# Thresholding one chunk a pair on Pool, and transposing the last queries on TensorE, in the opening of an attention and gated MLP kernel

## The chip, the cores and the metric

The kernel runs on one core of one Trainium2 chip. The metric is the device time of one execution in microseconds. The profile is one execution under the hardware profiler; its span is the time from its first to its last instruction, some 1.8 us shorter than the device time of the same execution.

A core has TensorE (PE in the profile; PEld are its weight loads), VectorE (DVE), ScalarE (ACT), GpSimd (POOL) and SyncE (SP, which issues most of the DMAs here). I write PE, Vector, Scalar and Pool. PE's results land in PSUM; e, the masks and the numerators of this kernel are in SBUF.

## The reference

```python
# attention: q, k, v are (8, 8, 576, 64); tau = 0.02
scores = scale * q @ k.T                        # 576 x 576 for each of 64 heads
scores = where(scores >= max(scores) - tau, scores, -1e9)
attn   = exp(scores - max(scores)); attn /= sum(attn)
x      = attn @ v                               # to (8, 576, 512)
# gated MLP with a spatial product
h = relu(x @ w_in); u, v = halves of h
v_n = normalise(v); v_s = w_spatial @ v_n + b
out = (u * v_s) @ w_out
```

An exponential is kept where it is at least exp(-tau), and is zero otherwise. That is the threshold. The kept values are the numerators.

## The kernel before

The 64 heads are worked through as 32 pairs. A pair has four chunks of 128 queries (c = 0 to 3), and its last 64 queries are put together with those of its neighbour as chunk 4 of the odd pair. So two pairs make nine steps, and there are 144 steps. A step computes the scores of one chunk (128 x 1152: two heads of 576 keys), takes the maximum, and exponentiates; the threshold of a chunk is applied one step later. The second half of the work, the MLP, enters at step 26. What comes before I call the opening, and what follows the body; the prediction counts pair 6 (steps 27 to 30) still to the opening.

```python
def on_act(c):
    return c in (2, 4)            # these chunks are thresholded by Scalar

def mask():                       # the chunk of the step before
    i, c, e = unmasked.pop()
    if c == 4:                    # last queries of two pairs
        dst = pts[i // 2] = ptr_ring[i // 2 % 2]
        nc.sync.dma_start_transpose(out=dst, in_=pr_ring[i // 2 % 2])
        return
    pt = p_ring[2 * (i % 2) + c // 2]
    if not on_act(c):             # chunks 0, 1, 3: Vector, e is fp32 in SBUF
        ef = e.rearrange("p h s -> p (h s)")
        nc.vector.scalar_tensor_tensor(out=pt[:, c % 2, :], in0=ef, scalar=ctau, in1=ef,
                                       op0=ALU.is_ge, op1=ALU.mult)
    if c % 2:                     # two chunks: numerators transposed by a DMA
        ...dma_start_transpose...

def step(i, c, fs):
    s = scores(i, c)              # PE into one of two PSUM score buffers
    ...                           # PE's and Scalar's small work of the step, fs[:2]
    nc.vector.tensor_reduce(out=nm, in_=s, axis=AX.X, op=ALU.max, negate=True)
    if on_act(c):                 # the bias instruction: 2 columns, SBUF to SBUF
        nc.vector.tensor_scalar(out=nm, in0=nm, scalar1=by, scalar2=float(tau),
                                op0=ALU.mult, op1=ALU.add)
    ...                           # Vector's divisions of fs[:2]
    e = ep.tile([P, 2, S], F32, name="e")       # ep has bufs=3
    ...                           # Scalar: exponentials of both heads from s into e
    if unmasked:
        mask()
    unmasked.append((i, c, e))
    ...                           # fs[2:]
```

Pool copies loaded q, k and v into working layouts, makes a small block-diagonal key tile (kd), and in the body normalises v.

## Time and profile before

| | before |
|---|---|
| three runs | 479.87 us (479.84 to 483.53) |
| span of the profile | 478.6 us |
| PE busy | 448.3 us, 94% |
| Vector busy | 418.0 us, 87% |
| Scalar busy | 382.2 us, 80% |
| Pool busy | 229.1 us, 48% |
| numerators to their transposes on the DMA queue, last queries | 16 transposes, 3.7 us each from issue to landing |

Busy time says how long an engine's instructions were under way, including the time in which a started instruction waits (the bias instruction shows 0.17 us in one place of this trace and 1.07 us in another, where Pool works at the same time).

### The profile page before, as it was taken

The numbers are of one execution on the slowest core, as the hardware profiler recorded it, in microseconds if no ns is written. First come the engines' busy times: TensorE is split into PE (matmuls) and PEld (weight loads), VectorE is DVE, ScalarE is ACT, GpSimd is POOL, SyncE is SP. The second block draws the span as 40 slices with busy tenths as digits, with TensorE's granted clock in tenths as the row PEclk, the third lists the DMA queues.
The fourth block names the chain that finished last, engine by engine and source line by source line (L and its number), as shares of the span: only waits on it lengthen the run. The fifth ranks groups of instructions, "written<-read, shape, count | busy, mean of one in ns | idle before, by whom it ended". The sixth has DMA issues, their size and how long they took to land.

```text
span 478.6 us, 9894 instructions
## 1 busy us (share of the span) xinstructions
PE 448.3 (94%) x3664; PEld 238.3 (50%) x3664; DVE 418.0 (87%) x563; ACT 382.2 (80%) x666; POOL 229.1 (48%) x403
## 2 busy tenths in 40 slices
PE   7788888889899999999999999999999999999995
PEld 4344444454554555554555545555554545545542
DVE  4999999989889997999889898899889998898573
ACT  4778777998879798788979898798978889797251
POOL 3462544784337553474427652475436743253021
PEclk9899999999999999999999999999999999999999
DMA  7999999979999799898988999997996999766523
GB/s 225 255 185 199 223 236 197 214 159 204 179 191 194 172 212 223 189 170 183 192 197 202 182 200 191 223 190 156 222 227 170 195 173 218 138 113 120 149 82 117
DMA packets 231120, 89.38 MB, mean 187 GB/s; under 512 B 200608, under 2 KB 225312, under 8 KB 231072
## 3 DMA queue, kind: packets, MB, share of 16 engines
q1 hardware_dynamic: 230416, 87.86, 87.2%
q8 instruction: 29, 0.48, 0.4%
q0 software_dynamic: 160, 0.52, 0.3%
q10 hardware_dynamic: 496, 0.36, 0.2%
q14 instruction: 19, 0.16, 0.1%
HBM read 33.31 MB, written 9.44 MB: 89 GB/s over the span
## 4 chain that ended last, share of the span: by engine, by line
PE 48%; DVE 23%; ACT 19%; issue 6%; DMA 2%; SPq 1%; POOL 0%; POOLq 0%; ACTq 0%; DVEq 0%
PE s L550 14%; DVE negm L586 10%; DVE p L567 8%; PE f L245 5%; ACT e L609 5%; PE s L545 4%; ACT e L603 4%; PE f L294 4%; PE f L519 4%; PE f L460 3%; ACT p L605 2%; ACT vrel L428 2%; PE f L490 2%; PE f L289 2%; ACT sq L442 1%
## 5 line engine op out<-in xcount | busy, mean ns | idle before, releaser
L586 DVE TENSOR_REDUCE negm<-s 128x2 f32<-128x1152 f32 x144 | 194.8, 1353 | 26.1 <-PE s L550 25.3
L550 PE MATMUL s<-qkT 64*128 64x512 f32 (+1 forms) x640 | 162.9, 639 | 0.0
L567 DVE SCALAR_TENSOR_TENSOR p<-e,ctau 128x1152 bf16<-128x1152 f32 x96 | 138.6, 1444 | 1.3 <-ACT e L609 1.2
L609 ACT ACTIVATE e<-s,negm 128x576 f32<-128x576 f32 x192 | 131.8, 741 | 7.1 <-DVE negm L586 6.8
L603 ACT ACTIVATE e<-s,negm 128x576 f32<-128x576 f32 x96 | 65.9, 738 | 20.9 <-DVE negm L590 11.6
L545 PE MATMUL s<-kd,qkT 128*128 128x128 f32 (+1 forms) x320 | 64.4, 304 | 15.6 <-ACT e L609 10.5
L268 POOL COPY kd<-qkT 64x64 f32<-64x64 f32 x62 | 31.7, 512 | 91.2 <-ACT qkT L263 89.4
L545 PEld LDWEIGHTS s<-kd,qkT 128*128 128x128 f32 (+1 forms) x320 | 44.4, 180 | 34.7 <-ACT e L609 20.2
L550 PEld LDWEIGHTS s<-qkT 64*128 64x128 f32 (+1 forms) x640 | 42.1, 174 | 18.3 <-issue 3.0
L436 POOL TENSOR_SCALAR nmean<-sm 128x1 f32<-128x1 f32 (+1 forms) x35 | 15.3, 437 | 69.7 <-ACT vrel L428 64.3
L294 PEld LDWEIGHTS <-pT 128*128 128x128 bf16 x1024 | 41.8, 97 | 7.3 <-issue 4.8
L294 PE MATMUL f<-v,pT 128*128 128x65 bf16 x992 | 44.9, 194 | 0.0
L136 POOL COPY qn<-ql 128x640 f32<-128x640 f32 x31 | 34.7, 1120 | 21.2 <-DMA ql<-in_k_dram 15.1
L605 ACT ACTIVATE p<-e 128x1152 bf16<-128x1152 f32 x32 | 37.3, 1165 | 1.0
L252 ACT COPY qkT<-f 128x512 f32<-128x512 f32 x31 | 18.2, 587 | 16.4 <-PE f L245 16.4
L490 PE MATMUL f<-wsT,vn 128*128 128x512 bf16 x125 | 31.1, 379 | 0.0
L448 POOL TENSOR_SCALAR vn<-vrel,rs,nm 128x512 bf16<-128x512 f32 (+1 forms) x34 | 28.7, 844 | 3.7
L289 PE MATMUL f<-v,pT 128*128 128x130 bf16 x124 | 27.2, 219 | 3.5 <-ACT qkT L252 1.6
L460 PE MATMUL f<-xT,w_in 128*128 128x512 bf16 x112 | 28.7, 380 | 0.9 <-DVE xn L303 0.8
L418 PE MATMUL f<-w_in,xT 128*128 128x512 bf16 x112 | 28.8, 380 | 0.0
L303 DVE TENSOR_TENSOR xn<-f,r 128x256 bf16<-128x256 f32 x62 | 26.3, 425 | 2.1
L428 ACT ACTIVATE vrel<-f 128x512 f32<-128x512 f32 (+1 forms) x34 | 20.1, 592 | 7.6 <-PE f L418 5.2
(165 smaller groups left out, 638.7 us busy)
## 6 DMA issues: line engine op xcount, KB each, us to landing
vl<-in_v_dram SPq DMA_DIRECT2D x16, 512.0 KB, 4.4
ql<-in_q_dram SPq DMA_DIRECT2D x15, 512.0 KB, 4.6
kl<-in_k_dram SPq DMA_DIRECT2D x15, 512.0 KB, 4.5
out_dram<-o SPq DMA_DIRECT2D x20, 256.0 KB, 3.4
uT<-in_moe_w_in_dram SPq DMA_DIRECT2D x3, 512.0 KB, 6.6
uT<-in_moe_w_spatial_dram SPq DMA_DIRECT2D x2, 576.0 KB, 5.0
vl<-in_v_dram SPq DMA_DIRECT2D x16, 64.0 KB, 4.1
pT<-p SPq DMA_TRANSPOSE x64, 5.5
```

The costliest lines, as they stand in the source:

```text
L136: nc.gpsimd.tensor_copy(out=t, in_=ld_ring[i // 2 % 2][w][:, 2 * (i % 2):2 * (i % 2) + 2].rearrange("p h c d -> p c h d"))
L289: nc.tensor.matmul(out=t[:, at:at + 130], lhsT=pt[:, 4, :], rhs=vt[:, 4:6, :].rearrange("p b d -> p (b d)"), start=True, stop=False)
L294: nc.tensor.matmul(out=t[:, at + 65 * h:at + 65 * h + 65], lhsT=pt[:, 5 * h + j, :], rhs=vt[:, 6 * h + j, :], start=False, stop=(h == 1 an ...
L460: nc.tensor.matmul(out=t, lhsT=w_in[:, m, f * P:(f + 1) * P], rhs=xts[b][:, m, 0:512], start=(m == 0), stop=(m == 3))
L490: nc.tensor.matmul(out=t, lhsT=vn[:, c, f * P:(f + 1) * P], rhs=wsT[:, c, 0:512], start=(c == 0), stop=(c == 4))
L545: nc.tensor.matmul(out=view(s[rows], 512, [[448, 2], [1, 64]]), lhsT=qks[n][:, 0, m], rhs=kd_ring[n % 2], start=True, stop=True)
L550: nc.tensor.matmul(out=s[rows, 1024 * h:1024 * h + 512], lhsT=qks[n][hs, 0, m], rhs=qks[n][hs, 1, 0:512], start=True, stop=True)
L567: nc.vector.scalar_tensor_tensor(out=pt[:, c % 2, :], in0=ef, scalar=ctau, in1=ef, op0=ALU.is_ge, op1=ALU.mult)
L586: nc.vector.tensor_reduce(out=nm, in_=s, axis=AX.X, op=ALU.max, negate=True)
L603: nc.scalar.activation(out=e[:, h, :], in_=s[:, h, :], func=ACT.Prelu, bias=nm[:, h:h + 1], scale=by, alpha=1e30)
L605: nc.scalar.activation(out=pr_ring[i // 2 % 2] if c == 4 else p_ring[2 * (i % 2) + c // 2][:, c % 2], in_=e.rearrange("p h s -> p (h s)"), ...
L609: nc.scalar.activation(out=e[:, h, :], in_=s[:, h, :], func=ACT.Exp, bias=nm[:, h:h + 1])
```

## The change

Vector is busy 98% of the time from 40 to 80 us, while Pool is more than half idle (8.60 and 8.90 us busy of 20). The change takes the threshold of chunk 0 from Vector in pairs 1 to 6 and gives it to Pool. Where Vector compares and multiplies in one instruction, the change uses two on Pool: a comparison into a bf16 mask `keep`, and a product. The change also takes three DMA transposes (the last queries of pairs 0 to 5) off the queue and does them on PE, nine 128 x 128 blocks each, in two jobs with a Scalar eviction each.

```diff
+    keep = const.tile([P, 1152], BF16, name="keep")
...
+    def pr_pe(m, half):
+        n0, n1 = ((0, 5), (5, 9))[half]
+        ...
+        def mm():
+            t = hold["t"] = bank16()
+            for n in range(n0, n1):
+                nc.tensor.transpose(out=t[:, (n - n0) * P:(n - n0 + 1) * P],
+                                    in_=pr_ring[m % 2][:, n * P:(n + 1) * P], identity=identb)
+        def ev():
+            nc.scalar.copy(out=ptr_ring[m % 2][:, n0:n1, :].rearrange("p n s -> p (n s)"),
+                           in_=hold["t"][:, 0:(n1 - n0) * P])
+        return "act", mm, ev
...
+            if i // 2 in r_on_pe:
+                return
             nc.sync.dma_start_transpose(out=dst, in_=pr_ring[i // 2 % 2])
...
-        if not on_act(c):
+        if c == 0 and 0 < i < 7:
+            ef = e.rearrange("p h s -> p (h s)")
+            nc.gpsimd.tensor_scalar(out=keep, in0=ef, scalar1=ctau, scalar2=1.0,
+                                    op0=ALU.is_ge, op1=ALU.mult)
+            nc.gpsimd.tensor_tensor(out=pt[:, c % 2, :], in0=ef, in1=keep, op=ALU.mult)
+        elif not on_act(c):
...
+    r_on_pe = {0: (9, 11), 1: (18, 20), 2: (25, 27)}
...
```

More of the change, by code (lines that the diff above doesn't have):

```diff
@@ L379, in x_pe @@
         return "act", mm, ev
+    def pr_pe(m, half):
+        n0, n1 = ((0, 5), (5, 9))[half]
+        hold = {}
+        def mm():
[7 more added lines that the diff above has]
+        return "act", mm, ev
     def ws_pe(c):
@@ L767 @@
         jobs.setdefault((29, 33, 34, 42, 44)[j], []).append((ws_pe, j))
+    for m, gs_ in r_on_pe.items():
+        for half, g in enumerate(gs_):
+            jobs.setdefault(g, []).append((pr_pe, m, half))
     with tc.manual_schedule():
```

## The prediction

> **What bounds the kernel now.** I read the page's slices first, then busy time by stretches, then the order of instructions on Vector, Scalar and Pool in the stretch that the change touches.
>
> ```profile
> PE   7788888889899999999999999999999999999995
> DVE  4999999989889997999889898899889998898573
> ```
>
> A slice is 12 us. TensorE (PE) reaches nine tenths and stays there only from about 110 us; before that Vector (DVE) is at nine tenths and more. By stretches, columns being PE, PEld, DVE, ACT, POOL busy us, clock, DMA share, GB/s:
>
> ```profile
> 40.00:60.00 20.00, 16.52 (x150) 9.19 (x148) 19.64 (x26) 16.24 (x25) 8.60 (x13) 1.00 0.92 207
> 60.00:80.00 20.00, 16.79 (x159) 9.03 (x157) 19.64 (x25) 14.52 (x23) 8.90 (x13) 1.00 1.13 217
> ...
> 360.00:400.00 40.00, 39.48 (x322) 20.34 (x319) 37.34 (x47) 34.91 (x64) 23.97 (x42) 1.00 0.90 192
> ```
>
> From 24 to 91 us, which is pairs 1 to 6, Vector is busy 98% (19.64 of 20) and PE about 83%; later PE is at 99%. So the kernel is a Vector-bound opening, then a PE-bound body. The body's PE work does not depend on when it starts, so I count a shift of the opening's end as a shift of the end. What moves the opening is therefore the question. One pair of it, pair 4, on Vector (start, duration, what):
>
> ```profile
> 57.77 1.41 DVE L567 SCALAR_TENSOR_TENSOR p<-e,ctau 128x1152 bf16<-128x1152 f32 x1
> 59.10 1.36 DVE L586 TENSOR_REDUCE negm<-s 128x2 f32<-128x1152 f32 x1
> 60.37 1.41 DVE L567 SCALAR_TENSOR_TENSOR p<-e,ctau 128x1152 bf16<-128x1152 f32 x1
> 61.70 1.35 DVE L586 TENSOR_REDUCE negm<-s 128x2 f32<-128x1152 f32 x1
> 63.08 0.71 DVE L590 TENSOR_SCALAR negm<-negm 128x2 f32<-128x2 f32 x1
> 63.70 1.83 DVE L567 SCALAR_TENSOR_TENSOR p<-e,ctau 128x1152 bf16<-128x1152 f32 x1
> 65.45 1.34 DVE L586 TENSOR_REDUCE negm<-s 128x2 f32<-128x1152 f32 x1
> ```
>
> The threshold at 60.37 is the one of chunk 0 that moves to Pool; the reduce at 61.70 and the tiny bias instruction at 63.08 belong to chunk 2; the threshold at 63.70 is that of chunk 1. Pool in the same time:
>
> ```profile
> 59.67 0.53 POOL L268 COPY kd<-qkT 64x64 f32<-64x64 f32 x2 [4.80 <-ACT qkT L263]
> 63.05 0.72 POOL L136 COPY qn<-ql 128x640 f32<-128x640 f32 x1 [2.85 <-DMA ql<-in_k_dram]
> 63.71 0.61 POOL L136 COPY kn<-kl 128x512 f32<-128x512 f32 x1
> 64.27 1.84 POOL L156 CAST v<-vl 128x640 bf16<-128x640 f32 x1
> ```
>
> The reader is to see the exclusion. The bias instruction takes 0.17 us when Pool is idle, here 0.71: it ends at 63.79, when Pool's copy of 63.05 ends (63.77). The threshold at 63.70 takes 1.83 instead of 1.41, because Pool's next copy (63.71 to 64.32) got in first; Pool's cast at 64.27 then takes 1.84 instead of 0.72, because the threshold holds it up. Elsewhere the same: bias instruction 51.89 to 52.91 against a Pool cast 51.85 to 52.89; 77.00 to 78.07 against 76.96 to 78.04. A reduce, which reads PSUM, is 1.35 us whatever Pool does.
>
> **What the Trainium skill says.** "SBUF — State Buffer", section "SBUF: two separate sides": Vector and Pool share a port pair, an exclusive lock held for the whole instruction, against Vector operations in a two-port mode or with two SBUF inputs. The trace agrees, with the numbers just given. "GPSIMD Engine Reference", section 3.1 "Elementwise — side-by-side cycle accounting": a Pool tensor_tensor of 2048 fp32 elements took 4497 ns, 1.96 times Vector's. This trace has Pool tensor_tensors of a few elements only, so nothing here confirms it. "TensorE: Matmul & The Clock Gate", "Part 4: PE-mode transpose": it lands in PSUM and needs a copy after; 275 to 390 ns each. Here four bf16 transposes in a row (the first at 59.14) are followed 0.23 us later by other work, so for throughput I use 0.06 us each.
>
> **The change, part by part.**
>
> Removed from Vector: six thresholds, in pairs 1 to 6. Each is 1.41 us on record and 1.33 us to the next instruction's start (60.37 to 61.70), so 8.0 us: the most that this part can give, 1.7% of 479.87.
>
> Added to Pool: six comparisons and six products of 1152 columns. Comparison: Pool's two-operation tensor_scalar on 512 columns with nothing in its way is 0.77 us (94.24 us), on one column 0.19; that is 1.13 ns a column, so 0.19 + 1151 x 0.00113 = 1.50 us. Product, estimated from the skill's figure scaled by columns: 4497 x 1152/2048 = 2.53 us. With a hop of 0.05 us, 4.1 us a pair, 24.5 us in all. Pool has that time (8.9 busy of 20), but holds the lock in it.
>
> When does it run? Chunk 0's exponentials of pair 4 end at 59.26 (57.89 + 1.37). Then come Scalar's small eviction (59.34) and the two kd copies, done at 60.20; both stand ahead in program order. So Pool compares from 60.20 to 61.70 and multiplies from 61.75 to 64.30: the end is 5.05 us after the exponentials. And Vector? The scores of chunk 2 wait for those same exponentials (two score buffers), and their last matmul ends at 60.87, so with the threshold gone the reduce starts at 60.9, not 61.70: the chain of exponentials, scores and reduce gives only 0.8 of the 1.33 us. The reduce ends at 62.25; the bias instruction then meets the product in flight and waits to 64.30, where before it ended at 63.79. If it should slip in between the two Pool instructions, the threshold of chunk 1 waits to the same 64.30.
>
> So I compare, for each pair, 5.05 us with the time from the end of chunk 0's exponentials to the end of the bias instruction before: 3.87, 3.98, 4.29, 4.53, 4.35 and 3.99 us for pairs 1 to 6 (28.75 - 24.88, 39.10 - 35.12, 52.91 - 48.62, 63.79 - 59.26, 78.07 - 73.72, 88.41 - 84.42). They sum to 25.0; six times 5.05 is 30.3. **The Pool part thus costs about 5.3 us instead of gaining 8.**
>
> Transposes on PE: 27 x 0.06 = 1.6 us of PE in a stretch where it idles a sixth; near nothing. Their six evictions cost Scalar 0.60 us (640 columns, like wsT at 88.37, next start 0.59 later) or 0.48 (512 columns, like xT at 46.76), 3.2 us. Those at steps 11, 20 and 25 stand before an exponential that waits for the bias instruction, and are hidden. Those at steps 9, 18 and 27 stand between the q eviction and chunk 0's exponentials, which start at once now (eviction from 57.34, exponentials at 57.89): they delay these by 0.60 + 0.60 + 0.48 = 1.7 us.
>
> Removed from the DMA queue: three transposes of 1.3 us of issue each. The queue is full from 40 to 82 us, but what it brings is early: Pool copies qn of pair 6 at 63.05 and PE transposes it at 69.73. The waits of PE for pT are 5.0 us in five places over the whole run. I give it 0.5 us.
>
> Given back: from 91 us on Vector has idle gaps (0.22, 0.78, 1.00 us by 98.5), so pair 6's loss is partly absorbed: 1.5 us. Sum: 5.3 + 1.7 - 0.5 - 1.5 = +5.0 us.
>
> **The rivals.** First, Pool is quicker than the estimate. At 3.0 us for both instructions the end comes at 3.95 us, below the mean of the six (4.17), so the pairs gain 1.3 us together, and with the evictions the change comes out at about even. For it: the mask is bf16, and a plain Pool copy of 1024 columns takes 1.04 us, 1 ns a column; against it: a two-input operation. Second, the change does what it is meant to: Vector's 8 us come off, less the 0.5 us a pair that the score buffers keep, minus the 1.7 us of evictions, about 3.5 us: 476 us. It needs Pool to finish within 2.1 us, or the lock to be rarely met. For it: the choice of exactly these pairs and steps looks tuned. Third, Pool's backlog makes it worse: its copies of qn and kn (0.66 + 0.56 us) then stand ready just when the threshold of chunk 1 wants the lock, and win it as at 63.71. In four of six pairs that adds 0.66 each, 2.6 us: about 487.5 us; with a product of 3 us, 490 us. Fourth, the DMA queue is the real bound of the opening (share 1.13): then three issues of 1.3 us would give up to 4 us, 476 us again. Against it: in the chain of waits the opening runs over Vector's reduces and thresholds, with one DMA stretch, 3.94 us.
>
> **Range and chances.** From +5.0 us I take 0.4 off for the first two rivals against the third: 484.5 us. The low end, 477.0, is the second rival nearly in full; the high end, 490.5, the third with a slow product. Faster by 2% needs 470.3 us, more than the whole 8 us: 3%. Slower by 2% is 489.5 us: 14%. Within: 83%.
>
> **What would show it.** Right: Pool comparisons near 1.5 us and products near 2.5 us; the bias instruction of chunk 2 in pairs 1 to 6 lengthened from 0.2-1.1 us to 1-2 us, ending with the product; Vector's busy time in 40 to 80 us still high, but from waiting; the first reduce of pair 7 (92.66 us now) later by about 5 us; the rest of the span unchanged in length. Wrong: a product under 1.5 us, or bias instructions that end before it, or pair 7 starting early. If pair 7 starts later and the end does not, then the claim that the opening's shift passes through is what failed.

## The result, and the profile after

The changed kernel took 501.29 us (median of 4 executions, 499.13 to 501.8) beside 480.66 us of the kernel before (479.84 to 483.53). The ratio is 1.0409, with a 95% interval from 1.0354 to 1.0465. A ratio here is the mean time of one kernel's fast runs over that of the other's of the same rounds, so it is not quite the ratio of the medians. The change made the kernel 4.1% slower. I had predicted 484.5 us, with 490.5 as the upper end.

The page's slices of the changed kernel, a slice being 12.5 us now:

```profile
PE   7768787859989999999999999999999999999995
DVE  5897898866988998799988998899898998899573
...
PEclk9887988997999999999999999999999999999998
```

And of the kernel before, the clock line that the prediction did not show:

```profile
PEclk9899999999999999999999999999999999999999
```

Neither PE nor Vector is near full through the first nine slices, so something holds both. The granted clock is also lower there. By stretches, with the same columns as in the prediction (PE, PEld, DVE, ACT, POOL busy us, clock, DMA share, GB/s):

```profile
40.00:60.00 20.00, 16.89 (x148) 9.52 (x146) 15.89 (x19) 14.42 (x23) 12.92 (x11) 0.93 0.81 182
60.00:80.00 20.00, 15.14 (x110) 7.21 (x107) 17.58 (x17) 13.24 (x20) 17.35 (x14) 0.84 0.73 174
...
360.00:400.00 40.00, 39.25 (x332) 21.18 (x333) 35.24 (x48) 33.93 (x61) 20.76 (x38) 1.00 1.02 199
```

Vector ran 36 instructions in 40 to 80 us, where it ran 51 before; Pool is busy for 30.3 us of these 40, where it was for 17.5. From 360 us on the two kernels look alike. The tile `keep` and its readers tell why (duration min, median, max in ns):

```profile
L587 POOL TENSOR_SCALAR keep<-e,ctau x6: 4174/4176/4178, 27.5 to 103.6; 128x1152 bf16<-128x1152 f32 x6
L589 POOL TENSOR_TENSOR p<-e,keep x6: 2361/2752/3144, 31.8 to 107.9; 128x1152 bf16<-128x1152 f32 x6
```

The product is 2.36 us where nothing obstructs it, near the 2.53 us that I estimated. The comparison is 4.18 us, and I had put it at 1.50. Pair 4 on Vector and then on Pool, the same pair as in the prediction (start, duration):

```profile
69.61 1.36 DVE L611 TENSOR_REDUCE negm<-s 128x2 f32<-128x1152 f32 x1
71.95 1.36 DVE L611 TENSOR_REDUCE negm<-s 128x2 f32<-128x1152 f32 x1 [0.98 <-PE s L567]
73.34 2.00 DVE L615 TENSOR_SCALAR negm<-negm 128x2 f32<-128x2 f32 x1
74.90 1.41 DVE L592 SCALAR_TENSOR_TENSOR p<-e,ctau 128x1152 bf16<-128x1152 f32 x1
76.23 1.34 DVE L611 TENSOR_REDUCE negm<-s 128x2 f32<-128x1152 f32 x1
```

```profile
70.52 0.52 POOL L269 COPY kd<-qkT 64x64 f32<-64x64 f32 x2 [2.33 <-ACT qkT L264]
71.14 4.18 POOL L587 TENSOR_SCALAR keep<-e,ctau 128x1152 bf16<-128x1152 f32 x1
75.40 3.14 POOL L589 TENSOR_TENSOR p<-e,keep 128x1152 bf16<-128x1152 f32 x1
```

The bias instruction asks at 73.34, while the comparison is under way, and ends at 75.34, when the comparison has ended (75.32). The threshold of chunk 1 follows at once and gets in before Pool's product, which therefore takes 3.14 us. In pairs 1 and 3 it is the other way round, because Vector has a division to do between bias instruction and threshold. Pair 1, on Vector and on Pool:

```profile
27.70 4.01 DVE L615 TENSOR_SCALAR negm<-negm 128x2 f32<-128x2 f32 x1
31.28 0.44 DVE L302 RECIPROCAL r<-f 128x4 f32<-128x4 f32 x1
31.78 0.42 DVE L304 TENSOR_TENSOR xn<-f,r 128x256 bf16<-128x256 f32 x1
32.12 3.24 DVE L592 SCALAR_TENSOR_TENSOR p<-e,ctau 128x1152 bf16<-128x1152 f32 x1
```

```profile
27.52 4.18 POOL L587 TENSOR_SCALAR keep<-e,ctau 128x1152 bf16<-128x1152 f32 x1
31.78 2.37 POOL L589 TENSOR_TENSOR p<-e,keep 128x1152 bf16<-128x1152 f32 x1
```

Here the bias instruction waits for the whole comparison (27.70 to 31.71), the product starts at 31.78 while Vector divides, and the threshold waits for the product too, from 32.12 to 34.15.

To see where the time comes from, I take the start of Vector's maximum in each of the 144 steps in both traces and subtract. The shift of the changed kernel against the one before, in us, at the first maximum of a pair:

| | pair 1, chunk 1 | pair 2 | pair 3 | pair 4 | pair 5 | pair 6 | pair 7 | pair 8 | step 102 | last step |
|---|---|---|---|---|---|---|---|---|---|---|
| start in the kernel before | 24.3 | 32.4 | 42.2 | 56.5 | 67.3 | 81.7 | 92.7 | 109.2 | 311.9 | 437.7 |
| shift of the changed kernel | -0.3 | +4.7 | +7.4 | +10.5 | +12.1 | +13.8 | +13.6 | +19.7 | +19.6 | +20.2 |

All of it arises before pair 8, and from there it hardly changes: the spans differ by 20.8 us (499.4 - 478.6).

### The profile page after: what moved, and what is told of

It is laid out like the page before. It is cut to its first block, busy times and chain, and to the rows that moved or that the text cites. A ratio compares the mean times of both kernels' runs of the same rounds, so it can differ in the third digit from the quotient of the medians.

```text
span 499.4 us, 9898 instructions
## 1 busy us (share of the span) xinstructions
PE 457.5 (92%) x3646; PEld 243.9 (49%) x3691; DVE 420.2 (84%) x557; ACT 385.5 (77%) x672; POOL 263.1 (53%) x415
## 4 chain that ended last, share of the span: by engine, by line
PE 52%; ACT 19%; DVE 16%; issue 5%; POOL 4%; DMA 2%; SPq 0%; POOLq 0%; ACTq 0%; DVEq 0%
PE s L567 16%; DVE negm L611 7%; ACT e L634 6%; PE s L562 5%; DVE p L592 5%; PE f L246 5%; PE f L295 4%; ACT e L628 4%; PE f L536 4%; PE f L477 3%; DVE negm L615 3%; PE f L507 2%; PE f L435 2%; PE f L290 2%; POOL keep L587 2%
## 5 line engine op out<-in xcount | busy, mean ns | idle before, releaser
L567 PE MATMUL s<-qkT 64*128 64x512 f32 (+1 forms) x640 | 168.1, 659 | 0.0
L634 ACT ACTIVATE e<-s,negm 128x576 f32<-128x576 f32 x192 | 131.7, 741 | 14.7 <-POOL p L589 5.0
L592 DVE SCALAR_TENSOR_TENSOR p<-e,ctau 128x1152 bf16<-128x1152 f32 x90 | 133.3, 1481 | 4.3 <-ACT e L634 4.2
L562 PE MATMUL s<-kd,qkT 128*128 128x128 f32 (+1 forms) x320 | 66.1, 311 | 23.4 <-ACT e L634 11.8
L269 POOL COPY kd<-qkT 64x64 f32<-64x64 f32 x62 | 28.0, 452 | 85.6 <-ACT qkT L264 83.8
L562 PEld LDWEIGHTS s<-kd,qkT 128*128 128x128 f32 (+1 forms) x320 | 45.6, 184 | 42.0 <-ACT e L634 21.0
L567 PEld LDWEIGHTS s<-qkT 64*128 64x128 f32 (+1 forms) x640 | 43.4, 180 | 19.0 <-issue 4.4
L453 POOL TENSOR_SCALAR nmean<-sm 128x1 f32<-128x1 f32 (+1 forms) x35 | 14.7, 419 | 67.8 <-ACT vrel L445 67.6
L137 POOL COPY qn<-ql 128x640 f32<-128x640 f32 x31 | 38.3, 1235 | 16.3 <-DVE negm L615 6.0
L465 POOL TENSOR_SCALAR vn<-vrel,rs,nm 128x512 bf16<-128x512 f32 (+1 forms) x34 | 27.3, 803 | 3.7
L246 PEld LDWEIGHTS f<-identf,qn 128*128 128x128 f32 x124 | 14.2, 150 | 26.9 <-POOL v L161 8.3
```

The source lines that it names most:

```text
L137: nc.gpsimd.tensor_copy(out=t, in_=ld_ring[i // 2 % 2][w][:, 2 * (i % 2):2 * (i % 2) + 2].rearrange("p h c d -> p c h d"))
L246: nc.tensor.transpose(out=t[:, c * P:(c + 1) * P], in_=nat[i][which][:, c, :], identity=identf)
L562: nc.tensor.matmul(out=view(s[rows], 512, [[448, 2], [1, 64]]), lhsT=qks[n][:, 0, m], rhs=kd_ring[n % 2], start=True, stop=True)
L567: nc.tensor.matmul(out=s[rows, 1024 * h:1024 * h + 512], lhsT=qks[n][hs, 0, m], rhs=qks[n][hs, 1, 0:512], start=True, stop=True)
L634: nc.scalar.activation(out=e[:, h, :], in_=s[:, h, :], func=ACT.Exp, bias=nm[:, h:h + 1])
```

## The experiments

Twelve kernels ran. The table gives the time, the ratio to the kernel before in the same rounds with its 95% interval, and the shift at pair 7, pair 8 and the last step from the one profile of each, made as above. The kernel before had medians of 479.22, 479.89 and 480.53 us in the rounds of the a, b and c runs; the b runs were on another chip than the a and c runs, so I compare runs of different letters by their ratios. Shifts under about 1.5 us mean little: at chunk 1 of pair 1 the profiles already differ from that of before by -1.7 to +1.2 us, the +1.2 being in a1, whose transposes all come later.

| run | us | ratio | pair 7 | pair 8 | last |
|---|---|---|---|---|---|
| changed kernel | 501.29 | 1.0409 (1.0354 to 1.0465) | +13.6 | +19.7 | +20.2 |
| a1, transposes alone | 481.31 | 1.0040 (1.0020 to 1.0060) | +1.9 | +1.8 | +1.8 |
| a2, Pool alone | 503.69 | 1.0501 (1.0475 to 1.0527) | +21.0 | +23.7 | +23.5 |
| a3, six forms | 496.40, one run | none | +8.8 | +15.1 | +15.4 |
| a4, comparison read by nobody | 501.07, one of four slow | 1.0418 (1.0375 to 1.0462) | +20.1 | +20.0 | +19.8 |
| b1, quick first instruction | 487.87 | 1.0145 (1.0106 to 1.0184) | +4.3 | +6.8 | +8.8 |
| b2, one quick instruction | 481.01 | 1.0015 (0.9981 to 1.0049) | -2.1 | -1.9 | +1.5 |
| b3, without pair 6 | 494.73 | 1.0301 (1.0257 to 1.0344) | +13.0 | +12.9 | +12.7 |
| b4, split bias, changed kernel | 499.20 | 1.0389 (1.0355 to 1.0424) | +10.8 | +16.8 | +18.5 |
| c3, four e buffers, changed kernel | 496.66 | 1.0333 (1.0294 to 1.0372) | +11.3 | +14.7 | +13.9 |
| c2, split bias, kernel before | 480.72 | 1.0004 (0.9972 to 1.0036) | -1.2 | -1.3 | +0.4 |
| c1, chunk 0 on Scalar | 481.29 | 1.0007 (0.9971 to 1.0043) | +0.2 | +0.1 | +2.3 |
| c5, split and half on Scalar | 481.19 | 1.0008 (0.9982 to 1.0034) | -0.8 | -1.0 | +0.2 |

My theory after the result was that Pool's slow comparison, and the port lock that it holds against Vector, make the loss. The rivals were the transposes, the late numerators with the buffers they hold, and the lowered clock.

### a1: the transposes alone

```diff
-        if c == 0 and 0 < i < 7:
+        if False:
```

> The transposes on PE alone, all thresholds on Vector. My theory (Pool's comparison of 4.18 us and the lock that it holds make the loss): close to the kernel before, 479 to 482.5 us, because only the evictions at steps 9, 18 and 27 (0.60 + 0.60 + 0.48 us) stand in the chain and three DMA transposes go away. Rival (the transposes and their evictions carry a large part of the loss, or the lowered TensorE clock comes from them): 485 us or more.

It took 481.31 us, 0.4% over the kernel before, which is 1.9 us (479.22 x 0.0040). So the transposes are slightly harmful and carry no large part of the loss. Its profile shows +1.2 us already at chunk 1 of pair 1, before the first of these transposes, and a granted clock of 0.87 in 20 to 40 us, so the trace does not give the evictions their 1.7 us; the time agrees with my net of 1.2 us for this part (1.7 - 0.5) within its interval.

### a2: Pool's thresholds alone

```diff
-    r_on_pe = {0: (9, 11), 1: (18, 20), 2: (25, 27)}
+    r_on_pe = {}
```

> The Pool thresholds alone, transposes left on the DMA queue. My theory: nearly the whole loss, 497 to 502 us, with comparisons of 4.2 us and the bias instructions of chunk 2 waiting 2 to 4 us. Rival (the transposes carry much of it): under 493 us.

It took 503.69 us, above what I expected, and more than the whole change with both its parts. Nearly the whole loss is Pool's. The surplus arises in pairs 5 and 6. In the changed kernel the transpose job of step 25 pushes pair 5's division behind the threshold of chunk 1, so that the threshold follows the bias instruction directly and asks for the port before Pool's product does (91.16 us, 1.41 us long). Here the division stands in between and the threshold loses:

```profile
90.05 2.00 DVE L615 TENSOR_SCALAR negm<-negm 128x2 f32<-128x2 f32 x1
91.61 0.44 DVE L302 RECIPROCAL r<-f 128x4 f32<-128x4 f32 x1
92.11 0.42 DVE L304 TENSOR_TENSOR xn<-f,r 128x256 bf16<-128x256 f32 x1
92.45 3.25 DVE L592 SCALAR_TENSOR_TENSOR p<-e,ctau 128x1152 bf16<-128x1152 f32 x1
```

That explains some 2 us at pair 6 (+15.8 against +13.8). The rest, from pair 6 to pair 7, I have not taken apart.

### a3: which form is slow

The edit gives the first Pool instruction of each pair another form, in short:

```text
pair 1: op0=is_ge, op1=mult      (scalars: ctau, 1.0, as in the change)
pair 2: op0=mult, op1=add        (ctau, 1.0)
pair 3: op0=max, op1=mult        (ctau, 1.0)
pair 4: op0=is_ge                (ctau, no second operation)
pair 5: op0=is_ge, op1=mult      (the constant 0.9802, 1.0)
pair 6: op0=subtract, op1=mult   (ctau, ctau)
```

> Changed kernel with another first Pool instruction in each pair (results wrong on purpose): pair 1 is_ge then mult, pair 2 mult then add, pair 3 max then mult, pair 4 is_ge alone, pair 5 is_ge then mult with the threshold as a constant, pair 6 subtract then mult with two pointer scalars. Theory A (the comparison is what is slow on Pool): 4.2 us in pairs 1, 4 and 5, about 1.5 us in pairs 2, 3 and 6, time about halfway, 485 to 493 us. Theory B (1152 columns or the conversion to bf16 are slow, whatever the operation): 4.2 us in all six, time near 500 us. Theory C (max is slow like is_ge): pair 3 also 4.2 us.

The six first instructions on Pool, in order of pairs:

```profile
25.93 4.18 POOL L588 TENSOR_SCALAR keep<-e,ctau 128x1152 bf16<-128x1152 f32 x1
...
40.76 1.22 POOL L590 TENSOR_SCALAR keep<-e,ctau 128x1152 bf16<-128x1152 f32 x1
...
55.33 4.18 POOL L592 TENSOR_SCALAR keep<-e,ctau 128x1152 bf16<-128x1152 f32 x1
...
69.09 3.21 POOL L594 TENSOR_SCALAR keep<-e,ctau 128x1152 bf16<-128x1152 f32 x1
...
82.67 4.10 POOL L596 TENSOR_SCALAR keep<-e 128x1152 bf16<-128x1152 f32 x1
...
98.82 4.25 POOL L598 TENSOR_SCALAR keep<-e,ctau 128x1152 bf16<-128x1152 f32 x1
```

None of my three theories holds as I stated it (theory C had pair 3 right, but not pair 6). It is not the comparison: max then mult takes the same 4.18 us and subtract then mult 4.25. It is not the width or the conversion: mult then add takes 1.22 us on the same tiles. Of these six, only mult then add is quick, and that is exactly the form of the normalising instruction from which I had scaled. Leaving out the second operation brings 3.21 us. Each form stands here once, in one execution; mult then add comes again in b1, with 1.22 us in most pairs. Why the forms differ is not shown. Its output is wrong, which doesn't matter for the time.

### a4: a comparison that nobody reads

```diff
+        if c == 0 and 0 < i < 7:
+            nc.gpsimd.tensor_scalar(out=keep, in0=still, scalar1=ctau, scalar2=1.0,
+                                    op0=ALU.is_ge, op1=ALU.mult)
         if not on_act(c):              # kernel before; still is a fixed fp32 tile
```

> The kernel before, with all thresholds kept on Vector, and in pairs 1 to 6 one more Pool comparison of 1152 columns at the place where the change puts it, on a fixed tile, its result read by nobody. Theory of the lock: Vector's threshold of chunk 0 waits for it, some 4 us in each of six pairs: 498 to 506 us. Rival (the loss comes from the late numerators, which hold buffers and delay the transposes after them): nobody waits for data here, so under 484 us.

It took 501.07 us, and its three fast executions (496.29 to 501.89 us) give a ratio of 1.0418, a loss as large as that of the change. Pool makes no numerator here and holds no e buffer; what is late is late by Vector's own waits. In pair 2, on Vector and on Pool:

```profile
37.38 1.36 DVE L591 TENSOR_REDUCE negm<-s 128x2 f32<-128x1152 f32 x1
38.65 4.97 DVE L572 SCALAR_TENSOR_TENSOR p<-e,ctau 128x1152 bf16<-128x1152 f32 x1
43.54 1.34 DVE L591 TENSOR_REDUCE negm<-s 128x2 f32<-128x1152 f32 x1
```

```profile
38.58 4.17 POOL L568 TENSOR_SCALAR keep<-still,ctau 128x1152 bf16<-128x1152 f32 x1
```

Vector's threshold asks at 38.65, 0.07 us after Pool has begun, and ends 0.87 us after Pool's end. So it is in pairs 2 to 5, where this threshold takes 4.97, 4.86, 4.89 and 4.60 us; in pair 1 the bias instruction waits instead (1.90 us). In the chain of waits of this run it is these instructions of Vector that stand there; Pool's own copies do not, up to pair 5. Pair 6 costs nothing: the comparison starts late, at 110.41, and the shift is +20.1 at pairs 6 and 7 and +20.0 at pair 8. So five instructions of 4.17 us on Pool are enough for 20 us. The lock alone can do it, but not in pair 6, where the changed kernel loses 6 us; c3 comes to that.

### b1: the prediction's sum at the size that it assumed

```diff
             nc.gpsimd.tensor_scalar(out=keep, in0=ef, scalar1=ctau, scalar2=1.0,
-                                    op0=ALU.is_ge, op1=ALU.mult)
+                                    op0=ALU.mult, op1=ALU.add)
```

> Changed kernel, the comparison replaced in all six pairs by mult then add (1.22 us in the run before; results wrong on purpose), product kept (2.37 us). This gives Pool nearly the 4.1 us a pair of my prediction. By the prediction's own sum the end of the product is 0.95 + 1.22 + 0.08 + 2.37 = 4.6 us after chunk 0's exponentials against 4.17 before: 6 x 0.45 = 2.7 us, and some 1.9 us for the evictions as measured alone: 482 to 486 us. If it stays over 490 us, the size of the comparison was not the failed step.

With 1.22 + 2.37 us on Pool it took 487.87 us, a ratio of 1.0145, which is 7.0 us (479.89 x 0.0145). Some 13.4 us of the loss (501.29 - 487.87, from two sets of rounds; 12.7 by the ratios) hang on the first instruction's form. The expected 482 to 486 was still too low. The trace gives 2.5 us of the surplus a place: the shift goes from +4.3 at pair 7 to +6.8 at pair 8. That is in pair 6, where Scalar waits 0.79 us for the buffer of which run c3 tells; the rest of the surplus I have not taken apart. Its output is wrong, which doesn't matter for the time.

### b2: one quick instruction on Pool

```diff
-            nc.gpsimd.tensor_scalar(out=keep, ...is_ge...mult)
-            nc.gpsimd.tensor_tensor(out=pt[:, c % 2, :], in0=ef, in1=keep, op=ALU.mult)
+            nc.gpsimd.tensor_scalar(out=pt[:, c % 2, :], in0=ef, scalar1=ctau, scalar2=1.0,
+                                    op0=ALU.mult, op1=ALU.add)
```

> Changed kernel with one Pool instruction a pair only, mult then add straight into the numerators (results wrong on purpose), 1.22 us: the change as it would be if Pool could threshold in one quick instruction. Theory: the lock is free again before the bias instruction asks for it, so the 8 us of Vector partly come off, bounded by the score buffers: 475.5 to 479 us. Rival (Vector is not what bounds the opening): as the transposes alone, 480 to 482 us.

It took 481.01 us, not told apart from the kernel before. The opening in its profile is 1.9 us shorter at pair 8, of which 0.8 were there at chunk 1 of pair 1, and near 314 us PE waited 2.04 us for a DMA in this one execution, after which the shift is +1.5. So even a Pool that thresholds in 1.22 us would have gained next to nothing, although Vector's busy time from 20 to 90 us falls from 68.08 to 60.85 us. This run keeps the transposes on PE: beside a1, which has them too, it is 0.25% quicker (1.2 us), with intervals that overlap. Its output is wrong, which doesn't matter for the time.

### b3: without pair 6

```diff
-        if c == 0 and 0 < i < 7:
+        if c == 0 and 0 < i < 6:
```

> Changed kernel without pair 6's Pool threshold. In the trace of the changed kernel the shift grows from 13.6 us at the first reduce of pair 7 to 20.2 us at its chunk 1, as pair 6's comparison comes only after the normalising chain of the second half on Pool and holds the e buffer that pair 7's exponentials wait for. If that is pair 6's own doing, this run loses 5 to 7 us of the 21: 494 to 496.5 us. Rival (an even share of each pair, a sixth of it): 497 to 498.5 us.

It took 494.73 us, inside the range of a loss that is pair 6's own. In the traces the shift at pair 8 falls from +19.7 to +12.9, so pair 6 costs 6.8 us, and the other five pairs with the transposes 12.9. By the ratios it is 1.1%, some 5.2 us; the profile of b3 is of one of its quicker executions.

### c3: a fourth e buffer

```diff
-    ep = ctx.enter_context(tc.tile_pool(name="ep", bufs=3))
+    ep = ctx.enter_context(tc.tile_pool(name="ep", bufs=4))   # in the changed kernel
```

> Changed kernel with four e buffers instead of three, nothing else. In its trace Scalar's exponentials of pair 6's chunk 3 (110.27 us) waited 3.84 us for the product on Pool that still read the e buffer they write. If the buffer is what makes pair 6 dear, most of the 6 us between the first reduces of pair 7 and pair 8 go: 494.5 to 497.5 us. If the lock and Pool's order do it alone: 500 to 502 us.

It took 496.66 us; at pair 8 the shift is +14.7 instead of +19.7. With three buffers, chunk 3 of a pair writes the e buffer that chunk 0 had, and Pool reads that one to the end of its product. In pair 6 of the changed kernel Pool first runs the normalising work that has just begun, so its comparison starts at 103.62 and its product ends at 110.24. Scalar waits:

```profile
110.27 1.37 ACT L634 ACTIVATE e<-s,negm 128x576 f32<-128x576 f32 x2 [3.84 <-POOL p L589]
```

Between pair 7 and pair 8 the shift grows by 3.4 us (+11.3 to +14.7) where it grew by 6.1 (+13.6 to +19.7), so the fourth buffer is worth 2.7 us there. It does not take the wait away: the buffer of chunk 0 now comes to be written one step later, by pair 7's first exponentials, and Scalar waits 2.01 us for the same product there (at 107.87 us). So a good part of what pair 6 still costs in this run may be the buffer too. The other 2.3 us, before pair 7, are partly two waits of 0.57 us of the same kind in pairs 2 and 4, and partly the difference at the start of the two profiles, -1.0 against -0.3 us at chunk 1 of pair 1. By the ratios the whole gain is 0.8%, some 3.6 us; this profile too is of a quick execution (494.91 us).

### b4 and c2: bias instructions that do not meet the lock

```diff
-            nc.vector.tensor_scalar(out=nm, in0=nm, scalar1=by, scalar2=float(tau), ...)
+            for h in range(2):
+                nc.vector.tensor_scalar(out=nm[:, h:h + 1], in0=nm[:, h:h + 1], scalar1=by,
+                                        scalar2=float(tau), ...)
```

> Changed kernel with Vector's bias instruction split into two of one column each. If the lock binds it through a two-port mode that needs an even number of columns, the split ones no longer wait (0.17 us each in pairs 1 to 6 instead of 1.4 to 4.0), chunk 2's exponentials start 2 to 4 us sooner, and Vector waits at chunk 1's threshold instead, which has two SBUF inputs; as everything on Vector is behind that one, the time falls by 3 to 8 us: 493 to 498 us. If the split ones wait as long, any Vector instruction that reads SBUF alone is held: 501 to 502 us.

> The kernel before with the bias instruction split into two of one column, which never waited for Pool in the run before (0.21 us for both, always). In the kernel before such waits came in about a dozen of 48 places, up to 1 us each, five of them in the opening: 0.5, 0.3, 0.85, 0.54 and 0.9 us. Theory (Vector bounds the opening, and a wait taken out there reaches the end): 1 to 2.5 us less, 477 to 479 us beside 479.9. Rival (Vector's chunk 1 threshold then waits for the same Pool instruction): no difference within 0.5 us.

In the changed kernel (b4) the two one-column instructions take 0.21 us together and never wait, also with a comparison under way; the wait moves to the next instruction with two inputs in SBUF, the threshold:

```profile
28.01 0.21 DVE L616 TENSOR_SCALAR negm<-negm 128x1 f32<-128x1 f32 x2
28.14 0.17 DVE L302 RECIPROCAL r<-f 128x4 f32<-128x4 f32 x1
28.35 0.42 DVE L304 TENSOR_TENSOR xn<-f,r 128x256 bf16<-128x256 f32 x1
28.69 4.30 DVE L592 SCALAR_TENSOR_TENSOR p<-e,ctau 128x1152 bf16<-128x1152 f32 x1
```

The time, 499.20 us, is little better than the changed kernel's and above my range. This fits the Trainium skill, "Advanced Engine Details and Errata", section "2x-2p Requirements", by which the two-port mode needs source and destination in SBUF and the "most non-unit major dimension" even in both, or odd, over 1 and equal in both: read as the columns here, two qualify and one does not. The runs show that two columns wait and one does not; that the mode is the reason they do not show. In the kernel before (c2) the same edit takes all of these waits out and changes nothing that could be told: 480.72 us, ratio 1.0004, though its interval still allows a gain of 1.3 us. The rival that I named there has the time right and the reason wrong: the thresholds behind the split instructions took 1.41 to 1.54 us in the opening, so the waits did not move to them.

### c1 and c5: the same relief of Vector by Scalar

```diff
-    def on_act(c):
-        return c in (2, 4)
+    def on_act(i, c):                                   # c1
+        return c in (2, 4) or c == 0 and 0 < i < 7      # c5: i in (2, 4, 6), and the split bias
```

> The change's aim by another engine: kernel before, threshold of chunk 0 of pairs 1 to 6 on Scalar in the form that chunk 2 already has (Prelu, then Exp of 1.17 us), none on Pool. It takes 8 us off Vector and puts six bias instructions on it (6 x 0.17 us) and 7 us on Scalar, which was busy 14.5 to 16.2 of 20 us in the opening. Theory (Vector bounds the opening, as long as nobody takes the lock for long): 476 to 479 us. Rival (Scalar's longer step becomes the bound, as the exponentials free the score buffers): 480 to 484 us.

> Split bias instructions and Scalar thresholds of chunk 0 in pairs 2, 4 and 6 only. If both effects add and Scalar has room for one more Exp every second pair: 475.5 to 478.5 us, the version that beats both kernels. If Scalar is the bound: not under the split alone.

Neither gains: 481.29 and 481.19 us, ratios 1.0007 and 1.0008. The stretch from 20 to 90 us (columns as before), first of the kernel before, then of c1:

```profile
20.00:90.00 70.00, 59.40 (x468) 31.31 (x469) 68.08 (x79) 55.78 (x89) 34.82 (x58) 0.98 1.04 210
```

```profile
20.00:90.00 70.00, 59.20 (x467) 31.14 (x464) 59.74 (x78) 61.60 (x95) 31.32 (x57) 0.98 1.03 203
```

Vector's busy time falls from 68.1 to 59.7 us of 70, Scalar's rises from 55.8 to 61.6, PE's stays at 59.4 and 59.2, and pair 8 begins at the same time (+0.1). So the opening is not bound by Vector's sum of work alone: taking 8.3 us off it, at the price of 5.8 on Scalar, gains nothing, and b2, which puts the work on Pool, points the same way. A kernel with these thresholds simply left out, and nothing added elsewhere, was not run. I ran no version that beats the kernel before.

## Why the prediction was wrong

**What bounds the kernel now.** The split into opening and body was right: in the changed kernel the shift is +19.7 us at pair 8 and +20.2 at the last step. (My reading of the slices was loose: PE's slice from 120 to 132 us is an 8 again.) "A Vector-bound opening" was wrong as a claim that relief of Vector is gained, though Vector is 98% busy there. c1 takes 8.3 us of busy time off Vector without a gain, and b2 7.2 us. What I had noted for pair 4, that scores, maximum and exponentials in two buffers follow right behind, points the right way, but it still promised 0.8 us a pair, 4.8 us in all, which neither run got. Which chain binds the opening once Vector is relieved is not shown.

**The exclusion.** Right, and it is the mechanism of the loss. The bias instruction, the threshold and Pool's instructions shut each other out as a whole (a4; in b4 the bias instruction of one column is the exception). That Pool could be quick enough only in about 4 us a pair was also the right comparison.

**The comparison of 1.50 us.** This is the step that failed, and the term of the sum that was mis-sized: it measured 4.18 us. I scaled a two-operation tensor_scalar by columns, but its operations were mult then add, and a3 shows that this form is quick (1.22 us at this width) while five others take 3.2 to 4.3. "Pool comparisons near 1.5 us" was the first thing that I said would show the step right or wrong. One of my signs of being wrong came true as well, "bias instructions that end before it": in pair 4 the bias instruction ended with the comparison at 75.34, and the product at 78.54. b1, with sizes below the assumed ones, comes to 487.87 us. That is inside my range by the range's width, not by the sum: by the prediction's own terms b1 should have lost some 2.4 us (2.7 from the pairs, 1.7 from the evictions, less 0.5 and 1.5), and it lost 7.0. So the comparison's size is the larger part of the error, some 13 of 20 us, and not all of it.

**The product of 2.53 us.** Right: 2.37 us where nothing obstructs it, longer only when Vector's threshold has the port.

**The sum.** Predicted +5.0 us; measured 20.8 us in the spans. By the traces pair 1 costs 5.0 us (from -0.3 to +4.7), pairs 2 to 5 cost 2.7, 3.0, 1.7 and 1.6, pair 6 together with what follows to pair 8 some 6. Two of the prediction's smaller terms failed besides. "If it should slip in between the two Pool instructions, the threshold of chunk 1 waits to the same 64.30": the bias instruction did slip in, but the threshold waited for the product in pairs 1 and 3 only; in pairs 2, 4 and 5 the threshold got the port between Pool's two instructions. "Pair 6's loss is partly absorbed: 1.5 us" had the wrong sign: there Pool's queue made the product late, and the three e buffers turned that into a wait of 3.84 us for Scalar. I had not looked at how long Pool would hold the buffer that it reads.

**The transposes.** Net 1.2 us predicted, 1.9 us (0.2 to 0.6%) measured: right within the noise, though the trace does not show where they cost it.

**The clock.** I had not foreseen it. In the chain of waits of the changed kernel the large matmuls of one chunk's scores take 1.96 to 2.01 us in places where 1.06 to 1.08 is usual, and PE's granted clock is 0.76 in 20 to 40 us against 0.93 before. Three such places from 38 to 113 us make some 3 us of the 20, an estimate from those durations. That the clock falls because PE idles is not shown.

## What to carry to other kernels

Do not scale an instruction's duration from another operation of the same kind: look for the same operations, and where the profile has none, treat the size as open and ask what the plan becomes if it is three times as long. When work moves to an engine that shares a lock with the one relieved, as Pool does with Vector here, add its whole duration to the relieved engine's path at the place where that one next wants the lock, and ask which buffers it keeps in the meantime. An engine that is 98% busy need not be the bound; relieve it once by some cheap and wrong edit and see whether the end moves before building the real thing.

## What the Trainium skill lacked or had wrong

- "GPSIMD Engine Reference", section 3: it gives tensor_tensor, a best case, and cycles per element by the number of operations, but no duration of a tensor_scalar by which operations it has. Here 128 x 1152 fp32 to bf16 took 1.22 us with mult then add, 3.21 us with is_ge alone, 4.10 to 4.18 us with is_ge then mult, 4.18 us with max then mult, and 4.25 us with subtract then mult. All but one have two operations, so the number does not tell them apart.
- "GPSIMD Engine Reference", section 3.1: it has no figure for a tensor_tensor with a bf16 input. My estimate from its fp32 figure, scaled by columns, was 2.53 us; an unobstructed product of an fp32 and a bf16 tile took 2.36 to 2.37 us.
- "SBUF — State Buffer", section "SBUF: two separate sides": the exclusive lock is confirmed, and so is that the one that starts first gets it. The page speaks of starting first and of issuing first, and does not say how that looks in a profile when both engines have been waiting: here the start that the profile shows decided, although Vector's threshold of pair 4 shows it (74.90) before the bias instruction ahead of it has ended (75.34). The threshold was served first in pairs 2, 4 and 5, where it starts 0.5 us before Pool's product (46.10 and 46.60, 74.90 and 75.40, 91.16 and 91.66), and the product in pairs 1 and 3, where Vector had other work between and the threshold starts 0.34 us after it.
- "TensorE: Matmul & The Clock Gate", "Part 4: PE-mode transpose": its 275 and 390 ns are for single bf16 transposes and are not their cost in a row of them; in the kernel before, each of four shows 219 ns, and other work followed 0.23 us after the start of the first, so a row costs 0.06 us each.
